# Packing head operands by halves of the sequence, with a block's sums and outputs sent two half steps later

## The chip, the cores and the metric

The kernel runs on one core of a Trainium2 chip. The metric is the device time of one execution in microseconds (us). The core has a matrix engine (TensorE, PE in the profile, with its weight loads apart as PEld), a vector engine (VectorE, DVE), a scalar engine (ScalarE, ACT), a further vector engine (GpSimd, POOL) and a synchronisation engine (SyncE, SP), which in this kernel issues all DMAs. Each engine has its own instruction stream, executed in order.

## The reference

Four residual layers, attention and Fourier mixing in turn, on x of 2048 rows by 640 columns, all in float32. Attention has 32 heads of 20 columns and a sliding window of 256 keys:

```
def _A_ref(x, wqkv, wo):
    H = 32; Dh = D // H; W = 256
    qkv = transpose((x @ wqkv).reshape(B, S, 3, H, Dh), 2, 0, 3, 1, 4)
    q, k, v = qkv[0], qkv[1], qkv[2]
    scores = einsum("bhqd,bhkd->bhqk", q, k) * (Dh ** -0.5)
    mask = (i - j >= 0) & (i - j < W)
    p = softmax(where(mask, scores, -1e9), axis=-1)
    o = einsum("bhqk,bhkd->bhqd", p, v)
    return transpose(o, 0, 2, 1, 3).reshape(B, S, D) @ wo

x = x + _A_ref(_layernorm(x), wqkv, wo)
x = x + _B_ref(_layernorm(x), dft matrices)   # real part of a DFT over both axes
x = x + _A_ref(_layernorm(x), wqkv, wo)
x = x + _B_ref(_layernorm(x), dft matrices)
```

## The kernel before

The sequence is cut into 16 blocks of 128 rows and into four quarters of 512. The 32 heads are cut into 8 quads of four. An attention layer has three parts. `before_heads` normalizes and transposes x and makes the values and the first projections. `heads` (L648) runs 128 steps, one for each quad and block. `after_heads` ends the output projection.

Projected queries and keys go to a DRAM tensor, `qk_d` (L566), as a high and a low part, 512 KB for each piece of 128 projected columns by one quarter. `pack` (L624) brings them back in the layout that the heads read, into `qp` and `kp`. Both are double buffers, by the quad's parity. For one quad and one quarter it makes 12 DMAs, 6 into `kp` and 6 into `qp`: 20 rows each, in two parts of 512 columns, 80 KB. `heads` issues them three to a step, over four steps (L834). The list `due` (L770) says in which step a pack begins: for quads 1 to 6, every four steps, 8 steps before the blocks of that quarter are first read.

A step t of `heads` does, in two half steps z = 0, 1 (two heads each):

- `s_head` for block s = t + 10: scores with the query on the rows (L673), to which DVE adds the mask and takes the largest of each row (L678, into `mc`);
- `t_pair` for block t: scores with the key on the rows (L701), then the exponential on ACT (L711) and two masks on POOL (L717, L721);
- `pv` for block v = t - 1: the product with the values (L736), copied to `ou` by ACT (L745);
- a piece of other matrix work, `fill`: a projection of a later quad, or from step 97 on a first part of the output projection (both L274).

The largest scores reach `t_pair` as a further row of its operand `qp`. Every four steps, in the half step z = 1 of a step t = 2 mod 4, `m_rows` (L683) transposes them (L686), ACT copies them to `mt` (L689), and at the end of that half step the code has SP send two DMAs `qp<-mt` (L691). They hold the rows of four blocks of 128. The rows of blocks 4 to 7 of a quad ("u1" below) stand two steps ahead of the quad's first, and `t_pair` reads them first in the quad's step 2; those of blocks 8 to 11 ("u2") stand in step 2 and are read first in step 6. Both leave four steps.

`finish` (L749) ends a group of four blocks of a quad. In half steps after it, `post` lets it send the softmax sums to `sm` (L755) and the raw output to `o_d` (L756), take the reciprocal on DVE (L758), and store that to `r_d` (L761). The numbers are `at` (L754). `ou` is a double buffer; it is written again five steps after its group has ended.

SP's order is the order of the program's code. SP waits in it where a DMA needs the result of an engine (`mt` of ACT, `sm` and `o_d` of ACT, `r_d` of DVE, `qk_d` of POOL), or needs an earlier DMA to have landed. Other DMAs of SP in the heads are `vq<-v_d` (L663, values), `x<-wqk` (L542, weights), `rr<-kr` and `rr<-ki` (L1459, a check of the Fourier matrices that runs beside the heads), and from step 87 on `x<-o_d`, `rr<-r_d` (L900, L906) and `big<-x` (L1012, the residual, which DVE adds at L1038).

Of the kernel before, what the change touches and what calls it, by code (L numbers as in the profile page):

```python
# [16 lines left out]
P = 128  # L17
# [5 lines left out]
NQ = H // 4  # L23
NSB = 4
# [49 lines left out]
class Net:  # L74
# [546 lines left out]
        self.prepare(4)  # L621


    def pack(self, quad, sb):  # L624

        todo = []
        cols = slice(sb * 512, (sb + 1) * 512)
        for c in range(160 * quad // P, -(-160 * (quad + 1) // P)):
            while self.slot is not None and c > 1 and (c, sb) not in self.packable:
                self.flush(("qk", c, sb))  # L630
                if self.heavy:
                    self.relieve()
                self.tick()

        def put(d, src):
            self.nc.sync.dma_start(d.bitcast(F32), src)

        for kind in (1, 0):
            for e in range(2):
                r0 = 160 * quad + 80 * kind + 40 * e  # L640
                dst = (self.qp, self.kp)[kind][quad % 2].rearrange("p (z s) -> p z s", z=2)
                for part, l in enumerate(((0, 1, 0), (0, 0, 1))[kind]):
                    b = 64 * e + 20 * part
                    src = self.qk[l, r0:r0 + 40, cols].rearrange("(z r) s -> r z s", z=2)
                    todo.append(lambda d=dst[b:b + 20, :, cols], src=src: put(d, src))
        return todo

    def heads(self, xsrc, xdst):  # L648
# [7 lines left out]
        def defer(d, fn):  # L656
            later.setdefault(now[0] + d, []).append(fn)
# [91 lines left out]
        def finish(quad, bk):  # L749
            ou = ous.pop((quad, bk))  # L750
            sm = pool.tile([P, 16], F32, name="sm", tag="sm")
            rc = pool.tile([P, 16], F32, name="rc", tag="rc")
            cols = slice(bk * 512, (bk + 1) * 512)
            at = (2, 9, 11) if quad < NQ - 1 else (1, 5, 6)  # L754
            self.post(at[0], lambda: nc.sync.dma_start(sm, ou[0:P:32, :]))  # L755
            self.post(at[0], lambda: nc.sync.dma_start(  # L756
                self.od[4 * quad:4 * quad + 4, :, cols].rearrange("h r s -> (h r) s"), ou))
            self.post(at[1], lambda: nc.vector.reciprocal(out=rc, in_=sm))  # L758

            def store():  # L760
                nc.sync.dma_start(  # L761
                    self.rd[bk, 4 * quad:4 * quad + 4, :].rearrange("h (a b) -> (h a) b", b=16), rc)
                self.post(2 if quad < NQ - 1 else 0, lambda: self.stored.add((quad, bk)))
            self.post(at[2], store)
# [4 lines left out]

        due = [(16 * q + (4 * j - AHEAD if q < NQ - 1 else LAST_DUE[j]),  # L770
                ((-(-160 * (q + 1) // P) - 1) * NSB + 2 * (j // 2) + 2) * per_piece, q, j)
               for q in range(1, NQ) for j in range(NSB)]
        self.xsrc = xsrc
        self.out = self.partials(xsrc)
        self.rest = self.late(xdst)
# [17 lines left out]
        def fill(n):  # L793

            k, size = 0, 1
            while k < size:
                r = more()
                if r == 0 and k == 0:
                    continue
                if r != 1:  # L800
                    return
                k += 1
                if k == 1:
                    left = self.left + 1
                    size = -(-left // max(1, round(left / n)))
            if self.left == 0:
                more()
                if self.lead:
                    relieve()
                elif self.heavy:  # L810
                    self.heavy.sort(key=lambda h: h[0] not in ROLES["m"])
                    self.relieve()
# [5 lines left out]
        for step in range(-LEAD, steps + 1):  # L818
# [11 lines left out]
            if due and s >= due[0][0]:  # L830
                while done[0] < due[0][1]:
                    fill(15)
                q, j = due.pop(0)[2:]
                for i, f in enumerate(self.pack(q, j)):  # L834
                    defer(i // 3, f)
                for f in later.pop(step, []):
                    f()
# [847 lines left out]
```

## Time and profile before

| | |
|---|---|
| time, median of 3 runs | 1399.29 us (1399.02 to 1400.3) |
| the profiled execution | 1401.8 us, its span 1400.1 us |
| steps of the heads, first attention layer | 163.3 to 541.2 us |
| steps of the heads, second attention layer | 852.8 to 1230.4 us |
| busy share of the span | PE 93%, DVE 70%, ACT 54%, POOL 51% |
| DMA, mean | 187 GB/s |
| DMAs `kp<-qk_d` and `qp<-qk_d` | 384 and 384, 80 KB each |

The busy shares are means over stages with different limits. The heads are 54% of the span, and a quad of 16 steps there takes 43.5 to 48.7 us where nothing but projections runs beside it (quads 1 to 5). Times below are from the span's start. In a line of the profile, `A <-B` names the buffer written and the one read, "x24" a count, and "<-" behind a wait what ended it. Q behind an engine's name (SPq) is its sequencer, where DMAs are issued.

### The profile page before, as it was taken

How to read it: one execution, taken by the hardware profiler on the slowest of the kernel's cores; microseconds unless marked ns; L12 is line 12 of the kernel's file. 1: busy time of each engine (PE TensorE's matmuls, PEld its weight loads, DVE VectorE, ACT ScalarE, POOL GpSimd, SP SyncE). 2: the span in 40 equal slices, each digit the busy share in tenths (PEclk: the TensorE clock that was granted, in tenths of full speed). 3: DMA queues.
4: the chain of work that ended last, by engine and by line, in shares of the span. 5: the costliest groups of instructions: out<-in, count | busy, mean ns of one | idle time of the engine just before them, and what ended most of it. 6: DMA issues, size and time to landing. Idle time of an engine off the chain costs nothing.

```text
span 1400.1 us, 37389 instructions
## 1 busy us (share of the span) xinstructions
PE 1307.4 (93%) x13350; PEld 1007.4 (72%) x13350; DVE 980.9 (70%) x3172; ACT 758.9 (54%) x1651; POOL 713.7 (51%) x1469
## 2 busy tenths in 40 slices
PE   6998999999999889899999999999999988988997
PEld 6898777776766777753689987777676777777445
DVE  6722788787788773877876148887787778658764
ACT  2322378777776564437423225777677755734460
POOL 4221687877777673210323236887777776622000
PEclk9999999999999999999999999999999999999999
DMA  5665576776778875417426646777777787561343
GB/s 192 217 216 158 174 205 201 209 217 206 214 213 245 211 208 143 156 54 241 170 99 193 207 154 195 206 209 202 211 217 214 220 234 219 170 217 46 118 146 144
DMA packets 174295, 261.48 MB, mean 187 GB/s; under 512 B 36306, under 2 KB 85586, under 8 KB 174100
## 3 DMA queue, kind: packets, MB, share of 16 engines
q1 hardware_dynamic: 174100, 259.00, 61.4%
q8 instruction: 108, 1.77, 0.6%
q14 instruction: 87, 0.71, 0.2%
HBM read 175.42 MB, written 82.31 MB: 184 GB/s over the span
## 4 chain that ended last, share of the span: by engine, by line
PE 35%; DMA 7%; DVE 4%; ACT 2%; POOL 2%; SPq 2%; issue 1%; ACTq 0%; DVEq 0%; POOLq 0%
PE banks L274 8%; PE banks L256 7%; PE banks L736 4%; PE banks L1383 3%; PE banks L701 3%; PE banks L1299 3%; PE banks L673 3%; DMA x<-o_d 1%; PE banks L1399 1%; ACT pt L711 1%; DMA qp<-mt 1%; DVE banks L678 1%; DMA big<-x_d 1%; DMA rr<-ki 1%; PE banks L1145 1%
## 5 line engine op out<-in xcount | busy, mean ns | idle before, releaser
L678 DVE CUSTOM_DVE_ANT_0 banks<-banks,mask 128x384 f32<-128x384 f32 (+2 forms) x1024 | 527.1, 557 | 136.3 <-PE banks L673 118.9
L711 ACT ACTIVATE pt<-banks 128x768 f32<-128x768 f32 (+2 forms) x512 | 394.3, 771 | 163.3 <-PE banks L701 115.3
L717 POOL TENSOR_SCALAR_AFFINE_SELECT pt<-pt 128x256 f32<-128x256 f32 x512 | 220.0, 430 | 161.5 <-ACT pt L711 140.3
L274 PE MATMUL banks<-big,wc 64*128 64x512 f32 x1920 | 280.0, 402 | 0.4 <-DVE pt L480 0.4
L701 PE MATMUL banks<-qp,kp 61*128 61x384 f32 (+2 forms) x1024 | 211.2, 383 | 36.8 <-DVE mc L678 18.5
L673 PE MATMUL banks<-kp,qp 60*128 60x384 f32 (+2 forms) x1024 | 212.2, 357 | 10.8 <-DVE mc L678 6.5
L736 PE MATMUL banks<-pt,vq 128*32 128x128 f32 x5760 | 213.0, 279 | 0.9 <-ACT pt L711 0.8
L274 PEld LDWEIGHTS banks<-big,wc 64*128 64x128 f32 x1920 | 196.1, 190 | 20.4 <-ACT x L586 2.7
L721 POOL TENSOR_SCALAR_AFFINE_SELECT pt<-pt 128x256 f32<-128x256 f32 x448 | 188.1, 420 | 0.0
L701 PEld LDWEIGHTS banks<-qp,kp 61*128 61x128 f32 x1024 | 108.8, 187 | 100.9 <-DVE mc L678 66.3
L736 PEld LDWEIGHTS banks<-pt,vq 128*32 128x32 f32 x5760 | 143.4, 110 | 50.3 <-issue 37.1
L673 PEld LDWEIGHTS banks<-kp,qp 60*128 60x128 f32 x1024 | 125.3, 189 | 40.3 <-DVE mc L678 23.4
L678 DVE DVE_READ_ACCUMULATOR2_ANT mc<- 128x1 f32 x1024 | 144.4, 141 | 0.0
L1466 POOL TENSOR_TENSOR rr<-rr 128x228 f32<-128x228 f32 (+3 forms) x113 | 74.7, 666 | 92.0 <-DMA rr<-ki 36.6
L745 ACT ACTIVATE ou<-banks 128x128 f32<-128x128 f32 (+2 forms) x288 | 73.3, 266 | 62.3 <-PE banks L736 56.4
L256 PE MATMUL banks<-qp,big 128*128 128x320 f32 x576 | 98.5, 316 | 1.0 <-POOL qp L382 1.0
L256 PE MATMUL banks<-qp,kp 128*128 128x320 f32 x384 | 88.4, 367 | 10.2 <-ACT big L1118 5.0
L228 POOL TENSOR_TENSOR c<-x,c 128x256 fp32r<-128x256 f32 x128 | 95.5, 753 | 0.0
L256 PEld LDWEIGHTS banks<-qp,big 128*128 128x128 f32 x576 | 88.4, 192 | 1.6 <-POOL qp L382 1.4
L256 PEld LDWEIGHTS banks<-qp,kp 128*128 128x128 f32 x384 | 65.9, 203 | 25.6 <-ACT big L1118 7.6
L274 PE MATMUL banks<-big,big 64*128 64x320 f32 x912 | 79.5, 310 | 0.2 <-ACT mt L689 0.2
L1153 POOL TENSOR_TENSOR rs<-mv,half 128x1 f32<-128x1 f32 x32 | 21.0, 655 | 112.6 <-DVE mv L1152 103.3
(168 smaller groups left out, 1805.9 us busy)
## 6 DMA issues: line engine op xcount, KB each, us to landing
qk_d<-c SPq DMA_DIRECT2D x80, 512.0 KB
kp<-qk_d SPq DMA_DIRECT2D x384, 80.0 KB
qp<-qk_d SPq DMA_DIRECT2D x384, 80.0 KB
o_d<-ou SPq DMA_DIRECT2D x64, 256.0 KB
v_d<-pt SPq DMA_DIRECT2D x16, 768.0 KB
vq<-v_d SPq DMA_DIRECT2D x64, 192.0 KB
rr<-ki SPq DMA_DIRECT2D x40, 228.0 KB
big<-x SPq DMA_DIRECT2D x26, 320.0 KB
```

The source lines that it names most:

```text
L228: eng.tensor_tensor(out=lo[..., c], in0=src[..., c], in1=hi[..., c].bitcast(F32), op=OP.subtract)
L256: self.nc.tensor.matmul(p, x, y, start=n == 0, stop=n == last)
L274: self.nc.tensor.matmul(ps[a], x[r], y[r], start=half + i == 0, stop=half == 1 and i == n - 1, skip_group_check=True)
L673: nc.tensor.matmul(p, qp[quad % 2][b:b + 60, z, qb * P:(qb + 1) * P], kp[quad % 2][b:b + 60, z, k0 * P:(qb + 1) * P], start=True, stop=True)
L678: nc.vector.tensor_tensor_reduce(out=p, in0=p, in1=self.mask[:, 384 - n * P:], scale=1.0, scalar=NEG, op0=OP.add, op1=OP.max, accum_out=mc ...
L701: nc.tensor.matmul(self.banks[:, banks[e], :n * P], kp[quad % 2][b:b + 61, z, kb * P:(kb + 1) * P], qp[quad % 2][b:b + 61, z, kb * P:(kb + ...
L711: nc.scalar.activation(pt[quad, kb][:, 2 * z:2 * z + 2, :n * P], self.banks[:, b0:b1 + 1, :n * P], AF.Exp, scale=SCALE)
L717: nc.gpsimd.affine_select(out=t[:, :, 0:P], in_=t[:, :, 0:P], pattern=[[0, 2], [1, P]], compare_op=OP.is_ge, fill=0.0, base=0, channel_mul ...
L721: nc.gpsimd.affine_select(out=t[:, :, 256:384], in_=t[:, :, 256:384], pattern=[[0, 2], [-1, P]], compare_op=OP.is_gt, fill=0.0, base=0, ch ...
L736: nc.tensor.matmul(self.banks[32 * h:32 * h + 32, bank, :P], vq[:, 96 * (kb % 4) + 21 * h:96 * (kb % 4) + 21 * h + 32], t[:, h, (qb - kb) ...
L745: nc.scalar.activation(ou[:, dst], self.banks[:, bank, src], AF.Copy)
L1466: eng.tensor_tensor(out=t[:, lo:hi], in0=t[:, lo:hi], in1=base.broadcast_to([P, hi - lo, w]), op=op)
```

## The change

`pack` takes a number n of quarters and makes one DMA over all of them. The quads 1 to 6 are packed in two halves of the sequence, each in the place in which its first quarter was packed before; quad 0, packed ahead of the steps, and quad 7 keep quarters. `finish` sends `sm` and `o_d` two half steps later, and takes the reciprocal and stores it one half step later, in all quads but the last.

```
-    def pack(self, quad, sb):
+    def pack(self, quad, sb, n=1):
         todo = []
-        cols = slice(sb * 512, (sb + 1) * 512)
-        for c in range(160 * quad // P, -(-160 * (quad + 1) // P)):
-            while self.slot is not None and c > 1 and (c, sb) not in self.packable:
-                self.flush(("qk", c, sb))
+        cols = slice(sb * 512, (sb + n) * 512)
+        for c, of in ((c, of) for c in range(160 * quad // P, -(-160 * (quad + 1) // P)) for of in range(sb, sb + n)):
+            while self.slot is not None and c > 1 and (c, of) not in self.packable:
+                self.flush(("qk", c, of))
...
-            at = (2, 9, 11) if quad < NQ - 1 else (1, 5, 6)
+            at = (4, 10, 12) if quad < NQ - 1 else (1, 5, 6)
...
-               for q in range(1, NQ) for j in range(NSB)]
+               for q in range(1, NQ) for j in range(0, NSB, 2 if q < NQ - 1 else 1)]
...
-                for i, f in enumerate(self.pack(q, j)):
+                for i, f in enumerate(self.pack(q, j, 2 if q < NQ - 1 else 1)):
```

The `flush` in `pack` is reached neither before nor after: every piece is stored by the time it is packed. So the engines other than SP keep their order, but for the reciprocal on DVE and for one place that follows from the outputs' later store, below.

The first place is SP's stream at the end of quad 1, from the `mt` of quad 2's blocks 0 to 3 (not shown) to the `mt` of its blocks 4 to 7 (the last row). Before:

```order
L636 DMA kp_573<-qk_d 20x2x512 x3
L1459 DMA rr_106<-kr 128x456
L636 DMA qp_122<-qk_d 20x2x512 x3
L663 DMA vq_101<-v_d 128x384
L636 DMA qp_122<-qk_d 20x2x512 x3
L542 DMA x<-wqk 128x640
L755 DMA sm<-ou_104 128x1x16
L756 DMA o_d<-ou_104 128x512
L761 DMA r_d<-rc 128x16
L636 DMA kp_1248<-qk_d 20x2x512 x3
L566 DMA qk_d<-c 128x2x512
L691 DMA qp_122<-mt 2x4x128 x2
```

After, the same stretch:

```order
L1459 DMA rr_106<-kr 128x456
L663 DMA vq_101<-v_d 128x384
L542 DMA x<-wqk 128x640
L636 DMA kp_1248<-qk_d 20x2x1024 x3
L761 DMA r_d<-rc 128x16
L755 DMA sm<-ou_104 128x1x16
L756 DMA o_d<-ou_104 128x512
L566 DMA qk_d<-c 128x2x512
L691 DMA qp_122<-mt 2x4x128 x2
```

Ahead of these two `mt` DMAs stood 19 DMAs, 12 of them packs; now 10 stand there, 3 of them packs, of twice the size. `sm` and `o_d` have moved behind `kp` and behind the reciprocal of the group before them.

The second place is the next stretch, up to the `mt` of quad 2's blocks 8 to 11. After:

```order
L1459 DMA rr_107<-kr 128x456
L636 DMA kp_1248<-qk_d 20x2x1024 x3
L566 DMA qk_d<-c 128x2x512
L636 DMA qp_1249<-qk_d 20x2x1024 x3
L663 DMA vq_99<-v_d 128x384
L636 DMA qp_1249<-qk_d 20x2x1024 x3
L1459 DMA rr_108<-kr 128x456
L761 DMA r_d<-rc 128x16
L755 DMA sm<-ou_105 128x1x16
L756 DMA o_d<-ou_105 128x512
L691 DMA qp_122<-mt 2x4x128 x2
```

This stretch had 12 packs of 80 KB before, and has 9 of 160 KB now. The two kinds of stretch alternate.

The third place is on PE, in step 97 of a layer (quad 6), where the first part of the output projection begins once `o_d` and `r_d` are stored:

```order
 L701 MATMUL banks<-qp_122,kp_573 128x384 x2
 L673 MATMUL banks<-kp_573,qp_122 128x384 x2
-L274 MATMUL banks<-big_5763,big_5764 128x320 x18
 L701 MATMUL banks<-qp_122,kp_573 128x384 x2
 L673 MATMUL banks<-kp_573,qp_122 128x384 x2
```

Each later group of this projection stands one step later, and at the end of the heads one group of nine L256 matmuls more stands behind the last step.

## The prediction

> **What bounds the kernel now.** I read the busy shares first, then who waits for whom on PE, then stretches of one quad each.
>
> ```profile
> PE 1307.4 (93%) x13350; PEld 1007.4 (72%) x13350; DVE 980.9 (70%) x3172; ACT 758.9 (54%) x1651; POOL 713.7 (51%) x1469
> ...
> PE banks L701 <- DMA qp<-mt: 7.1, 5, 3.0
> ...
> PE banks L701 <- DMA qp<-mt: 6.5, 3, 2.6
> ...
> PE banks L701 <- DMA qp<-mt: 1.6, 1, 1.6
> ```
>
> The first row is the page's, the others are PE's waits (us in all, times, longest) in quads 1 to 5 of the first attention layer, in those of the second, and in quad 6 of the first. PE bounds the heads; what it waits for there is the transfer of the largest scores, `mt`. The stretches of quads 1 to 5, both layers:
>
> ```profile
> 207.00:250.80 43.80, 43.04 (x618) 32.68 (x614) 36.83 (x138) 34.01 (x70) 34.42 (x75) 1.00 0.71 204
> 250.80:298.10 47.30, 44.60 (x618) 33.75 (x614) 36.20 (x137) 34.45 (x72) 37.04 (x81) 0.96 0.75 212
> 298.10:342.00 43.90, 42.96 (x616) 32.73 (x612) 36.58 (x138) 33.84 (x70) 34.31 (x75) 1.00 0.70 211
> 342.00:389.80 47.80, 44.35 (x610) 32.94 (x604) 36.92 (x138) 33.87 (x70) 35.96 (x79) 0.96 0.74 211
> 389.80:435.60 45.80, 43.31 (x602) 31.51 (x598) 38.12 (x139) 34.26 (x67) 36.41 (x78) 1.00 0.74 228
> 896.70:940.20 43.50, 42.94 (x616) 32.50 (x612) 36.37 (x137) 34.04 (x70) 35.83 (x83) 1.00 0.71 203
> 940.20:986.50 46.30, 44.59 (x618) 33.81 (x614) 36.36 (x138) 34.58 (x72) 37.07 (x84) 0.96 0.73 206
> 986.50:1033.70 47.20, 44.57 (x618) 33.63 (x614) 36.53 (x138) 33.83 (x70) 36.48 (x85) 0.96 0.79 218
> 1033.70:1077.20 43.50, 42.67 (x610) 31.58 (x606) 36.39 (x137) 33.91 (x70) 35.52 (x83) 1.00 0.72 209
> 1077.20:1125.90 48.70, 45.35 (x600) 33.32 (x596) 38.07 (x140) 34.37 (x67) 36.77 (x79) 0.93 0.73 218
> ```
>
> A row gives the length in us, then busy us of PE, PEld, DVE, ACT and POOL, the granted clock, the DMA share and GB/s. Four quads are alike: 43.80, 43.90, 43.50 and 43.50, mean 43.7. The other six take 283.1 us together, 21.0 more than six times that mean. One such stall, in quad 2 of the first layer, on ACT, SP and PE:
>
> ```profile
> 248.61 0.25 ACT L689 ACTIVATE mt<-banks 16x128 fp32r<-16x128 f32 x1
> ...
> 247.50 1.81 SPq L636 DMA_DIRECT2D qp<-qk_d  x3
> 249.36 0.36 SPq L542 DMA_DIRECT2D x<-wqk  x1
> 250.86 0.61 SPq L755 DMA_DIRECT2D sm<-ou  x1
> 251.51 0.48 SPq L756 DMA_DIRECT2D o_d<-ou  x1
> 252.09 0.37 SPq L761 DMA_DIRECT2D r_d<-rc  x1
> 253.02 1.05 SPq L636 DMA_DIRECT2D kp<-qk_d  x3
> 254.17 0.39 SPq L566 DMA_DIRECT2D qk_d<-c  x1
> 254.89 1.22 SPq L691 DMA_DIRECT2D qp<-mt  x2
> ...
> 258.05 0.69 PE L701 MATMUL banks<-qp,kp 61*128 61x384 f32 x2 [2.16 <-DMA qp<-mt]
> ...
> 255.50:266.50 11.00, 8.84 (x97) 6.58 (x95) 6.84 (x25) 6.30 (x13) 5.08 (x13) 0.84 0.81 242
> ```
>
> `mt` was ready at 248.86, and SP came to it at 254.89, a lag of 6.0 us. Of these, 3.7 are issuing (0.45 left of the packs, 0.36, 0.61, 0.48, 0.37, 1.05, 0.39), the other 2.3 are waits. PE idled 2.16 us, so **a lag of 3.9 us would have cost nothing**. Behind the stall the clock fell: 0.84 over 11.0 us is 1.8 us more. 2.16 and 1.8 make 3.9, near the 3.6 by which this quad exceeds 43.7. So SP's stream is the limit, through `mt` alone.
>
> The clock can be read another way. The Trainium skill's page "TensorE: Matmul & The Clock Gate", Part 1, has the gate fall after an idle window of about 3.4 us; by that a stall of 2.16 us would cost only itself, and the removable time would be 7.1 + 6.5 = 13.6 us in place of 21.0. The row with 0.84 speaks against it, and the sum goes by the rows.
>
> **The change part by part.**
>
> *Fewer packs.* The rows of the change show 19 DMAs ahead of the `mt` of blocks 4 to 7 before, 12 of them packs, and 10 now, 3 of them packs. The price of one:
>
> ```profile
> L636 SPq DMA_DIRECT2D kp<-qk_d x384: 273/336/1382, 56.5 to 1177.4; - x192
> ...
> L566 SPq DMA_DIRECT2D qk_d<-c x80: 359/387/2012, 42.6 to 1146.3; - x80
> ...
> kp<-qk_d SPq DMA_DIRECT2D x384, 80.0 KB
> ...
> qk_d<-c SPq DMA_DIRECT2D x80, 512.0 KB
> ```
>
> The three numbers are least, median and largest ns of one issue. An 80 KB pack costs 336 and a 512 KB store 387, so a pack of 160 KB is taken at 0.34 us; it lies between the two. Six quads lose 24 of 48 packs each in two layers, 288 of 768: 97 us of issuing on SP, 2.0 us in each four steps of some 10.9. That time is on the path only through the lag.
>
> *The lag now, blocks 4 to 7.* The three packs ahead of `mt` need no engine's result of that moment, so SP can issue them early; its gate is `r_d`, whose reciprocal stands three half steps, 4.1 us at 43.7 / 32 = 1.37 each, ahead of the copy to `mt`. From the gate: 0.37 + 0.61 + 0.48 + 0.39 = 1.9 us of issuing, with the 2.3 us of waits kept 4.2. The lag is 0.1 us; with twice the waits 2.4. Both are under 3.9, so the stalls at step 2 of a quad go: **-21.0 us**, bounds 0 and -21.0.
>
> *The lag now, blocks 8 to 11.* Their `mt` stands at the end of the packs. 16 DMAs take 9 x 0.34 + 2 x 0.40 + 0.39 + 0.34 + 0.37 + 0.61 + 0.48 = 6.1 us (`vq` taken as a pack), and the `mt` pair ahead 1.2: 7.3 of 10.9. But the transfers bunch. Four steps now hold 12 x 160 KB of packs, two `qk_d` of 512, and about 0.8 MB of others (`o_d`, `vq` with 128 x 384 x 4 bytes, a check or two): 3.7 MB, and the next four steps 0.8. The most that a stretch of the heads shows is
>
> ```profile
> 449.40:465.50 16.10, 13.79 (x205) 11.39 (x201) 10.20 (x39) 9.13 (x18) 10.60 (x22) 0.89 0.94 289
> ...
> L1459 SPq DMA_DIRECT2D rr<-kr x36: 327/402/1470, 184.3 to 759.2; - x36
> ...
> o_d<-ou SPq DMA_DIRECT2D x64, 256.0 KB
> ...
> rr<-kr SPq DMA_DIRECT2D x36, 228.0 KB
> ```
>
> 289 GB/s at a share of 0.94. At that rate 3.7 MB take 12.8 us, 1.9 over their four steps, so this lag is 0 to 1.9 us, under 3.9. I take **+2.0** for a few short waits; bounds 0 and the slower rival below.
>
> *Sums and outputs later.* From `sm`'s place to the reciprocal there are now six half steps (8.2 us) in place of seven, and from `o_d`'s to the next writing of `ou` seven in place of nine. What waited before:
>
> ```profile
>   DVE rc L758: 2.4, 5
> ```
>
> DVE waited 2.4 us in five of 64 reciprocals, where SP lagged; no such wait of ACT for `o_d` stands among its waits. The lag that goes, up to 6.0 us, is more than the one or two half steps given up. Cost 0, bounds -2.4 and +2.4; it is hidden by DVE's 30% of idle time.
>
> *The output projection's first part one step later.*
>
> ```profile
> 438.97 1.48 PE L274 MATMUL banks<-big,big 64*128 64x320 f32 x18
> ...
> 541.45 1.14 PE L256 MATMUL banks<-big,big 128*128 128x320 f32 x6
> 542.43 0.60 PE L256 MATMUL banks<-big 128*128 128x320 f32 x3
> ...
> DVE big L1038 <- DMA big<-x: 1.4, 1, 1.4
> ...
> DVE big L1038 <- DMA big<-x_d: 2.6, 1, 2.6
> ```
>
> Step 97 loses 1.48 us of PE work; behind the last step nine L256 more take 1.6 (541.45 to 543.03). If step 97 shortens in full this is 0, if not +1.6 a layer: I take **+1.5** for both, bounds 0 and +3.2. DVE's first addition of the residual waited 1.4 and 2.6 us for its load and held PE; the addition comes a step later, 2.9 us, and the load doesn't: **-3.0**, bounds 0 and -4.0.
>
> *Sum.* -21.0 + 2.0 + 1.5 - 3.0 = -20.5 us: from the profiled execution's 1401.8 (span 1400.1) to 1381.3. The median of the runs, 1399.29, is 2.5 below that execution, so I predict **1379**.
>
> **The rivals.**
>
> *Half of it stays.* SP's 2.3 us of waits grow with the larger transfers, and the `mt` of blocks 4 to 7 still lags by 4 to 5 us in some quads. For: SP does wait on landings,
>
> ```profile
> SPq L755 <- DMA rr<-kr: 5.3, 5, 2.2
> ```
>
> Against: 9 of 19 DMAs are gone from ahead of it. Half of 21.0 and no gain at the residual: -10.5 + 3.5 = -7, 1392.
>
> *The change doesn't do what it says.* If the lag is made by bytes in flight, not by issues, it stays, since the bytes are the same: 1399 to 1402 with the moved matmuls. Against: 3.7 of the 6.0 us were issuing.
>
> *Slower: the bunched packs hold up the `mt` of blocks 8 to 11.* Place: step 6 of quads 0 to 5, 12 in all. Price: 4.1 us each, as in the quad of 47.80, so 49 us; with -21.0 + 1.5 that gives 1399 + 30 = 1429. It decides from a lag of 3.9 us. It would come so if a pack, with its 20 rows, runs on 10 of the 16 DMA engines: 1920 / 10 + 1800 / 16 = 305 KB on each of these, at 289 / 16 = 18.1 GB/s 16.9 us, 6.0 over the four steps. Against: in the row 255.50:266.50 these engines would have had 96 + 1700 / 16 = 202 KB (12 packs of 80 KB in its 2.66 MB) in 11.0 us at a share of 0.81, so they could do 22.7 GB/s, and 305 KB take 13.4 us, 2.5 over. The Trainium skill's page "DMA: Bandwidth & Descriptors", "Why a DMA increments its semaphore by 16 and not by 1", has such a rule: a DMA takes the largest number of engines up to 16 that divides its outer sizes, the lowest-numbered ones. No row of this profile shows the engines apart, so this keeps a chance.
>
> **How the numbers follow.** The forecast gets 0.66, half of it 0.14, no effect 0.09, the slower rival 0.11. The low end takes -21.0, -4.0, the 1.6 us of quad 6, and 1.8 us of clock behind each of these three: -32, 1367. The high end takes in the rival that keeps half and most of no effect, and leaves the slower one out: 1367 to 1398. A measurement of this kernel tells 0.2%, 2.8 us, from no change: faster 0.80, same 0.09, slower 0.11.
>
> **What would show it.** Right: all ten stretches near 43.7 us at a clock of 1.00; PE's wait for `qp<-mt` under 4 us in all; 480 packs; in SP's stream `mt` issued within 2 us of the copy. L1038's wait for its load gone. Wrong: waits of L701 for `qp<-mt` at step 6 in place of step 2, a DMA share over 0.95 in every second four steps, ACT's L745 waiting for `o_d<-ou`, or more than 5 us of DVE waiting for `sm`.

## The result, and the profile after

The changed kernel takes 1413.65 us (median of 20 runs, 1401.78 to 1423.27), the kernel before 1403.11 us (median of 20 runs, 1397.51 to 1415.8). The ratio is 1.0053, 95% interval 1.0031 to 1.0075: **slower by half a per cent**, where 1379 was predicted. The difference is small, but the interval doesn't contain 1, and e9 below repeats it. The profiled execution of the change took 1420.27 us, span 1418.5, so it lies 6.6 above its own median.

The page of the changed kernel, busy shares and the DMA queue (packets, MB, share of 16 engines):

```profile
PE 1315.4 (93%) x13350; PEld 1008.8 (71%) x13350; DVE 979.2 (69%) x3172; ACT 759.3 (54%) x1651; POOL 710.1 (50%) x1469
...
q1 hardware_dynamic: 159700, 258.98, 62.7%
```

The averages hardly moved. The waits did (us in all, times, longest), after:

```profile
DVE rc L758 <- DMA sm<-ou: 30.9, 18, 3.9
...
ACT ou L745 <- DMA o_d<-ou: 24.5, 14, 3.6
...
PE banks L701 <- DVE mc L678: 40.8, 54, 3.8
```

PE's wait for `qp<-mt`, 15.2 us in nine places before, is not among its waits any more. In its place DVE waits for `sm` (2.4 us before), ACT for `o_d` (nothing before), and PE for DVE, 18.5 us before:

```profile
PE banks L701 <- DVE mc L678: 18.5, 33, 2.6
```

Stretches of the changed kernel (columns as in the prediction): quads 1 to 5 of the first layer as a whole and of the second, then quad 5, which grew most, and quad 6, of the first layer and of the second.

```profile
207.50:446.40 238.90, 222.43 (x3042) 164.47 (x3038) 184.45 (x686) 170.77 (x349) 177.83 (x387) 0.96 0.76 203
907.30:1145.80 238.50, 221.87 (x3040) 164.05 (x3036) 183.41 (x686) 170.77 (x349) 180.56 (x409) 0.97 0.75 204
...
395.10:446.40 51.30, 45.74 (x602) 33.50 (x598) 38.44 (x139) 34.47 (x67) 35.20 (x77) 0.93 0.71 184
446.40:502.20 55.80, 49.77 (x748) 40.13 (x744) 43.55 (x150) 32.27 (x62) 37.43 (x81) 0.97 0.78 220
...
1092.60:1145.80 53.20, 46.05 (x600) 33.47 (x596) 38.47 (x140) 34.36 (x67) 35.46 (x78) 0.94 0.70 183
1145.80:1198.90 53.10, 47.97 (x750) 38.80 (x746) 43.63 (x150) 32.40 (x62) 37.56 (x81) 1.00 0.83 231
```

The same two stretches of quads 1 to 5 before:

```profile
207.00:435.60 228.60, 218.26 (x3042) 163.61 (x3038) 184.65 (x686) 170.43 (x349) 178.14 (x385) 0.99 0.73 213
896.70:1125.90 229.20, 220.12 (x3040) 164.85 (x3036) 183.71 (x686) 170.72 (x349) 181.68 (x409) 0.97 0.74 211
```

Quads 1 to 5 were to take about 19 us less and took 19.6 more (457.8 to 477.4). Quad 6 took 8.0 less (58.9 and 58.0 before, 55.8 and 53.1 now). Of the other 6.8 us of the span's 18.4, 2.9 and 3.3 lie behind the last step of the two layers, by the records, where in each nine more matmuls of the output projection stand now. The bytes per second fell, 203 and 204 for 213 and 211, though the packs are larger.

One new stall, in quad 4 of the first layer. The timeline of SP, DVE, ACT and PE (start, busy us, instruction; in brackets the idle time before it and what ended it):

```profile
351.31 1.60 SPq L636 DMA_DIRECT2D qp<-qk_d  x3
353.01 0.35 SPq L663 DMA_DIRECT2D vq<-v_d  x1
353.65 2.02 SPq L636 DMA_DIRECT2D qp<-qk_d  x3
356.58 0.34 SPq L761 DMA_DIRECT2D r_d<-rc  x1
358.65 0.62 SPq L755 DMA_DIRECT2D sm<-ou  x1
360.13 0.34 SPq L756 DMA_DIRECT2D o_d<-ou  x1
360.94 1.38 SPq L691 DMA_DIRECT2D qp<-mt  x2
...
364.81 0.25 DVE L758 RECIPROCAL rc<-sm 128x16 f32<-128x16 f32 x1 [3.85 <-DMA sm<-ou]
...
365.31 0.34 ACT L745 ACTIVATE ou<-banks 128x127 f32<-128x127 f32 x2 [3.26 <-DMA o_d<-ou]
...
365.64 0.69 PE L701 MATMUL banks<-qp,kp 61*128 61x384 f32 x2 [3.28 <-DVE mc L678]
```

What SP waited for in 350 to 361 us, and the stretch behind the stall:

```profile
SPq L636 <- DMA qk_d<-c: 1.8, 2, 1.1
SPq L755 <- DMA qp<-qk_d: 1.7, 1, 1.7
SPq L761 <- DMA rr<-kr: 0.8, 1, 0.8
SPq L756 <- DMA qp<-qk_d: 0.8, 1, 0.8
...
364.80:371.60 6.80, 5.96 (x49) 4.60 (x51) 4.08 (x16) 3.06 (x8) 4.95 (x8) 0.50 0.77 223
```

SP is to issue `sm`, whose data has long been there, and waits 1.7 us for a pack to land, with which `sm` has nothing to do. The pack is the one issued at 351.31. Behind it stand `vq`, `r_d` and five more packs: `sm` is the eighth DMA after it. By the trace's records that pack landed at 358.59, 0.06 us before `sm` was issued. In these records this holds for all of SP's DMAs, 1687 before and 1399 after: each signals its end on one of eight semaphores in rotation, and never were more than seven under way when another was issued. **SP waits until the DMA eight places earlier has landed.** A late `sm` stops DVE in its order for 3.85 us, DVE holds up `mc`, PE waits 3.28, and the clock is 0.50 over the next 6.8 us. The late issue isn't all of it: `sm` itself took 6.1 us to land here, where 3.9 was the median before.

Over quads 1 to 5, SP's time in issuing fell from 351 to 252 us by the trace's records. The rows of its waits for transfers add up to 57.5 us in 128 waits before and 169.3 in 237 after. Of the whole span, before:

```profile
SPq L636 <- DMA kp<-qk_d: 6.5, 26, 0.4
...
SPq L761 <- DMA qp<-qk_d: 3.8, 9, 0.8
```

After:

```profile
SPq L636 <- DMA kp<-qk_d: 33.6, 64, 1.4
...
SPq L755 <- DMA qp<-qk_d: 19.0, 21, 2.3
...
SPq L761 <- DMA qp<-qk_d: 16.7, 17, 2.6
```

So 99 us of issuing were saved and 112 us of waits for landings came. The packs land later: by the records, 8.4 us (median) after their issue for `qp` and 4.9 for `kp`, where those of 80 KB took 4.5 and 3.4. The transfers beside them also do: `sm` 5.4 for 3.9, `r_d` 6.4 for 3.5.

### The profile page after: what moved, and what is told of

It is laid out like the page before. It is cut to its first block, busy times and chain, and to the rows that moved or that the text cites. A ratio compares the mean times of both kernels' runs of the same rounds, so it can differ in the third digit from the quotient of the medians.

```text
span 1418.5 us, 37024 instructions
## 1 busy us (share of the span) xinstructions
PE 1315.4 (93%) x13350; PEld 1008.8 (71%) x13350; DVE 979.2 (69%) x3172; ACT 759.3 (54%) x1651; POOL 710.1 (50%) x1469
## 3 DMA queue, kind: packets, MB, share of 16 engines
q1 hardware_dynamic: 159700, 258.98, 62.7%
## 4 chain that ended last, share of the span: by engine, by line
PE 35%; DMA 6%; DVE 4%; POOL 2%; ACT 2%; issue 2%; SPq 1%; POOLq 0%; DVEq 0%; ACTq 0%
PE banks L274 8%; PE banks L256 7%; PE banks L736 4%; PE banks L701 3%; PE banks L1383 3%; PE banks L1299 3%; PE banks L673 3%; DMA sm<-ou 2%; DVE banks L678 1%; PE banks L1399 1%; DMA rr<-ki 1%; ACT pt L711 1%; POOL pt L717 1%; PE banks L1145 1%; DMA qk_d<-c 1%
## 5 line engine op out<-in xcount | busy, mean ns | idle before, releaser
L717 POOL TENSOR_SCALAR_AFFINE_SELECT pt<-pt 128x256 f32<-128x256 f32 x512 | 216.6, 424 | 171.0 <-ACT pt L711 154.4
L736 PE MATMUL banks<-pt,vq 128*32 128x128 f32 x5760 | 216.2, 280 | 2.8 <-ACT pt L711 1.5
L673 PE MATMUL banks<-kp,qp 60*128 60x384 f32 (+2 forms) x1024 | 208.5, 355 | 10.9 <-DVE mc L678 7.8
L721 POOL TENSOR_SCALAR_AFFINE_SELECT pt<-pt 128x256 f32<-128x256 f32 x448 | 184.1, 411 | 0.0
L673 PEld LDWEIGHTS banks<-kp,qp 60*128 60x128 f32 x1024 | 121.7, 190 | 41.2 <-DVE mc L678 25.9
L256 PE MATMUL banks<-qp,big 128*128 128x320 f32 x576 | 100.0, 319 | 1.0 <-POOL qp L382 1.0
L256 PE MATMUL banks<-qp,kp 128*128 128x320 f32 x384 | 89.7, 370 | 10.4 <-ACT big L1118 4.9
L256 PEld LDWEIGHTS banks<-qp,big 128*128 128x128 f32 x576 | 89.7, 194 | 1.6 <-POOL qp L382 1.4
L256 PEld LDWEIGHTS banks<-qp,kp 128*128 128x128 f32 x384 | 66.8, 205 | 26.4 <-ACT big L1118 7.5
```

The costliest lines, as they stand in the source:

```text
L256: self.nc.tensor.matmul(p, x, y, start=n == 0, stop=n == last)
L673: nc.tensor.matmul(p, qp[quad % 2][b:b + 60, z, qb * P:(qb + 1) * P], kp[quad % 2][b:b + 60, z, k0 * P:(qb + 1) * P], start=True, stop=True)
L717: nc.gpsimd.affine_select(out=t[:, :, 0:P], in_=t[:, :, 0:P], pattern=[[0, 2], [1, P]], compare_op=OP.is_ge, fill=0.0, base=0, channel_mul ...
L721: nc.gpsimd.affine_select(out=t[:, :, 256:384], in_=t[:, :, 256:384], pattern=[[0, 2], [-1, P]], compare_op=OP.is_gt, fill=0.0, base=0, ch ...
L736: nc.tensor.matmul(self.banks[32 * h:32 * h + 32, bank, :P], vq[:, 96 * (kb % 4) + 21 * h:96 * (kb % 4) + 21 * h + 32], t[:, h, (qb - kb) ...
```

## The experiments

Each kernel was run in five rounds beside the kernel before. "Places" are the half steps at which `sm` and `o_d` are sent, the reciprocal taken, and the reciprocal stored. Waits are us of PE for `qp<-mt`, DVE for `sm`, ACT for `o_d`, in the one profiled execution of each kernel; these executions lie between 7.6 us below (e8) and 8.2 above (e17) the median of their kernel, so small differences between waits say nothing. The letters of the theories are explained in each expectation: A and L blame the packs that stand at once in SP's stream, B and S the shorter way from `sm` and `o_d` to their users, C says that a wait taken away turns up at the next one, D, P and W blame the transfers themselves (their size, their rows, the engines' time).

| kernel | packs | places | ratio to before (95%) | waits |
|---|---|---|---|---|
| before | 80 KB, 3 a step | 2, 9, 11 | 1 | 15.2, 2.4, 0 |
| e9, the change again | 160 KB, 3 a step for 4 steps | 4, 10, 12 | 1.0060 (1.0032 to 1.0088) | 0.7, 30.5, 22.4 |
| e1 | as the change | 2, 9, 11 | 1.0158 (1.0116 to 1.0199) | 1.3, 39.4, 3.3 |
| e2 | as before | 4, 10, 12 | 1.0105 (1.0065 to 1.0145) | 20.5, 9.8, 11.8 |
| e3 | as the change | 4, 12, 14 | 1.0075 (1.0042 to 1.0107) | 7.0, 0, 12.9 |
| e5 | 160 KB, 3 every second step for 8, from 2 steps earlier | 2, 9, 11 | 0.9939 (0.9905 to 0.9973) | 19.5, 0, 0 |
| e6 | as e5 | 4, 10, 12 | 1.0032 (1.0004 to 1.0060) | 10.9, 20.4, 15.1 |
| e7 | 80 KB in rows of 4096 bytes, 3 a step for 8, from 2 steps earlier | 2, 9, 11 | 1.0055 (1.0033 to 1.0077) | 6.6, 3.5, 0 |
| e8 | 80 KB in rows of 2048 bytes, else as e7 | 2, 9, 11 | 1.0066 (1.0046 to 1.0087) | 5.8, 4.9, 0 |
| e10 | as the change | 2, 10, 12 | 1.0105 (1.0056 to 1.0155) | 10.9, 27.3, 17.5 |
| e11 | as e5 | 2, 10, 12 | 0.9921 (0.9885 to 0.9956) | 19.6, 0.6, 0 |
| e12 | 160 KB, 2 a step for 6, from 2 steps earlier | 2, 9, 11 | 0.9916 (0.9887 to 0.9946) | 3.8, 11.5, 0 |
| e13 | as e12, from 4 steps earlier | 2, 9, 11 | 1.0168 (1.0118 to 1.0218) | 22.5, 15.0, 0 |
| e14 | as the change, issued by GpSimd | 4, 10, 12 | 1.0564 (1.0528 to 1.0601) | 0.7, 0, 0.3 |
| e15 | as e12 | 2, 10, 12 | 0.9849 (0.9807 to 0.9891) | 9.1, 2.2, 2.0 |
| e16 | as the change, from 2 steps earlier | 2, 9, 11 | 1.0144 (1.0106 to 1.0182) | 24.2, 0.2, 0 |
| e17 | 160 KB, 2 a step for 6, from the change's place | 2, 9, 11 | 1.0252 (1.0207 to 1.0298) | 2.6, 1.3, 0 |
| e18 | as before | 2, 10, 12 | 1.0034 (1.0006 to 1.0063) | 18.3, 0.2, 0 |
| e19, e15 again | as e12 | 2, 10, 12 | 0.9830 (0.9804 to 0.9855) | 8.6, 4.1, 0.8 |

### Each half of the change alone, and a later reciprocal (e1, e2, e3)

e1 keeps the halves and puts the places back; e2 keeps quarters and takes the new places; e3 is the change with the reciprocal two half steps later still.

```
e1  -            at = (4, 10, 12) if quad < NQ - 1 else (1, 5, 6)
    +            at = (2, 9, 11) if quad < NQ - 1 else (1, 5, 6)
e2  -            at = (2, 9, 11) if quad < NQ - 1 else (1, 5, 6)     (of the kernel before)
    +            at = (4, 10, 12) if quad < NQ - 1 else (1, 5, 6)
e3  -            at = (4, 10, 12) if quad < NQ - 1 else (1, 5, 6)
    +            at = (4, 12, 14) if quad < NQ - 1 else (1, 5, 6)
```

> Halves as in the change, but sm, o_d, the reciprocal and r_d at their old places (2, 9, 11). Theory A (the bunched transfers of a half make SP fall behind at the end of each burst, wherever sm stands in the code): SP comes to sm at about the same time as in the changed kernel, since the last packs still stand ahead of it, and the reciprocal stands half a step earlier: DVE waits 25 to 45 us for sm in all, time 0.3% to 1.2% over before. Theory B (the later place of sm is what costs): sm goes out 2.7 us earlier, DVE waits under 8 us for it, the stalls on mt at step 2 stay away, time 1.0% to 1.5% under before.

> Quarters as before, with sm, o_d, the reciprocal and r_d at the new places (4, 10, 12). Theory A: no bunching; SP lags 3 to 6 us as before, and sm has one half step (1.4 us) less: DVE waits 5 to 20 us for sm, the stalls on mt at step 2 stay, time 0 to 0.8% over before. Theory B: the later place alone costs what the change costs and more, DVE waits 30 us or more for sm, time 1% to 2% over before.

> The change with the reciprocal and the store of r_d two half steps later still (4, 12, 14): sm gets 2.7 us more before DVE asks for it, SP's load stays the same. Theory A and B: the DVE waits for sm fall from 30.9 to under 10 us, and with them the stalls at step 5 of a quad; time 0.5% to 1.5% under the changed kernel. A rival C (the stalls at step 5 come from ACT's wait for o_d or from the mt of blocks 8 to 11, which land just as late, and DVE's wait only stands first): the stalls move to L745 or to L701 behind mt at step 6, time as the changed kernel's within 0.4%.

Either half alone loses, by 1.6% and 1.1%; together they lose 0.5%. So the loss is not that of the later places: with halves these make it smaller. Of the two expectations theory A has the waits right (DVE for `sm` 39.4 us in e1 and 9.8 in e2, where the stalls on `mt` stay), but both kernels lost more than it had (0.3 to 1.2% and 0 to 0.8%); theory B falls with e1. In e1, the waits:

```profile
DVE rc L758 <- DMA sm<-ou: 39.4, 20, 4.4
```

All the halves' gain is there (PE waits 1.3 us for `mt`), and DVE's waits for `sm` take more than that. e3, which doesn't compute the reference's result (where it departs wasn't found) and keeps the number of DMAs, leaves DVE no wait for `sm`; ACT's for `o_d` falls to 12.9, and PE's for `mt` comes back with 7.0. Part of the wait comes out at other DMAs of the stream. The time as a whole stays, but not for that reason: by the records quads 1 to 5 take 466.2 us where the change takes 477.5, much as theories A and B have it, and quad 7 takes 57.3 and 57.4 us where it takes 48.8 and 48.7. In quad 7 PE waits once in each layer for an exponential, first layer and second:

```profile
PE banks L736 <- ACT pt L711: 6.8, 1, 6.8
```

```profile
PE banks L736 <- ACT pt L711: 7.7, 1, 7.7
```

So e3's total doesn't show that a stall moves whole to the next wait. What makes quad 7's stall was not followed.

### Packs spread out, and the later places on top (e5, e6, e11)

e5 begins two steps earlier and issues three packs in every second step, with the places of before. e6 and e11 differ from it in the places only.

```
-        due = [(16 * q + (4 * j - AHEAD if q < NQ - 1 else LAST_DUE[j]),
+        due = [(16 * q + (4 * j - AHEAD - 2 if q < NQ - 1 else LAST_DUE[j]),
...
-                    defer(i // 3, f)
+                    defer((2 if q < NQ - 1 else 1) * (i // 3), f)
```

> Halves, but their 12 DMAs go three in every second step over eight steps, beginning two steps earlier, with sm, o_d, the reciprocal and r_d at their old places (2, 9, 11). SP's issues and the bytes are then even. Theory A: lags of SP stay under 3 us, waits of DVE for sm under 8 us, of PE for mt under 4 us, time 1.0% to 1.8% under before. A rival D (a transfer of 160 KB is itself the cost, since it lands later than two of 80 KB): the waits stay as in the changed kernel, time 0 to 1% over before.

> Packs of 160 KB, three in every second step over eight steps, begun two steps earlier, and the sums and outputs at (4, 10, 12) as in the change. Theory A (SP's queue is the limit, later sums let the qp<-mt transfers pass): PE's wait for qp<-mt falls from 19.5 us of the spread kernel with (2, 9, 11) to under 10, and the time to 1390 to 1398. Theory C (the later places shift the stall to DVE's wait for sm and ACT's for o_d): these waits come back with over 10 us, 1402 to 1412.

> The spread kernel (three packs of 160 KB in every second step, sums sent at 2) with the reciprocal and its store at 10 and 12 in place of 9 and 11. Theory S: no waits for sm there already, so nothing but SP's order changes: r_d goes later, the mt behind it earlier; PE's wait for qp<-mt below 19.5 us, ratio 0.988 to 0.995. Theory C: 0.994 to 1.003.

e5 is faster than before, with the same 160 KB packs, and DVE doesn't wait for `sm` nor ACT for `o_d`. So halves as such don't lose, and theory D falls; it matters how closely they follow each other, and where (e12 to e17 below). It isn't theory A as written either: PE's waits for `mt`, under 4 us by it, are 19.5, and the gain is 0.6% where it had 1.0 to 1.8. With the change's places (e6) the waits come back, as theory C has it:

```profile
DVE rc L758 <- DMA sm<-ou: 20.4, 16, 2.9
...
ACT ou L745 <- DMA o_d<-ou: 15.1, 12, 2.8
```

Here the two half steps that `sm` and `o_d` give up cost 0.9% (0.9939 to 1.0032). With `sm` and `o_d` left at 2, the later reciprocal and store alone (e11) cost nothing: 0.9921, with PE's waits for `mt` as in e5 (19.6).

### The length of a row (e7, e8)

The packs of the change move in rows of 4096 bytes instead of 2048, and their packets took more of the DMA engines' time (62.7% for 61.4%) with the same bytes. e7 and e8 cut each pack of e5 by its two groups of heads, three of 80 KB in a step for eight steps; e8 keeps `qk_d` by quarters in DRAM, so that the same 80 KB move in rows of 2048 bytes.

```
e7  +                    for z in range(2):
    +                        src = self.qk[l, r0 + 20 * z:r0 + 20 * z + 20, cols]
    +                        todo.append(lambda d=dst[b:b + 20, z, cols], src=src: put(d, src))
e8  -        self.qk = dram.tile([2, 2 * D, S], F32, name="qk_d")
    +        self.qk = dram.tile([2, NSB, 2 * D, 512], F32, name="qk_d")
```

> Halves of the sequence, but each pack of 160 KB cut in two by its two groups of heads: 80 KB each, 24 for a half, in rows of 4096 bytes, issued three in a step over eight steps, begun two steps earlier; sums and outputs at (2, 9, 11). Count, size and rate of the packs are those of before; what differs is the length of a row (4096 for 2048 bytes) and the order. Theory P (a row of 4096 bytes costs more than two of 2048): the first queue's share of the 16 engines stays at 62.5 to 65%, all landings are later than before, and the time is 0.5 to 1.5% above that of the kernel of this call that has rows of 2048 bytes. Theory A (the change lost by sending 3.8 MB in four steps, the length of a row is nothing): the two kernels agree within 0.3%, both lie within 0.5% of before (1396 to 1410), and the share is 61.4%.

> As the kernel with packs of 80 KB in rows of 4096 bytes, with one difference: the rows that are packed lie in DRAM by quarters of the sequence, so that the same 80 KB go in rows of 2048 bytes. Theory P: the packets are as before (mean about 105 ns, first queue's share 61 to 62%), the time is 0.5 to 1.5% below its partner's, ratio to before 0.995 to 1.003. Theory A: equal to its partner within 0.3%.

The page's DMA queue, e7 and then e8:

```profile
q1 hardware_dynamic: 162580, 259.00, 61.5%
```

```profile
q1 hardware_dynamic: 174100, 259.00, 62.2%
```

1412.55 and 1413.79 us: the length of a row changes nothing, and theory P falls. The two agree as theory A has it, but both lie outside its range, at 0.6% above before. The Trainium skill's page "Perfetto Trace Analysis", "DMA Optimizations", recommends batching small transfers into larger ones, such as 2 KB into 4 KB or 8 KB, for throughput. It speaks of whole transfers; the row within a transfer of 80 KB is another matter, and there no gain shows, in time or in the queue's share. Against e5, which has half as many DMAs with the same bytes, the two lose 1.2 and 1.3%. That the number of packs makes this is not shown: the last packs of a half also stand a step later in e7 and e8 than in e5. What they lose by shows in PE's wait for the packs themselves, `qp<-qk_d`, 16.7 us in e7 and 15.7 in e8, with e5's at 3.5.

> The change itself, so that it and the others stand against the same runs of before. All theories: 1.003 to 1.0075 of before, 1404 to 1418.

The change, measured again beside these, gave 1.0060, within its bounds.

### Sending the sums early (e10)

```
-            at = (4, 10, 12) if quad < NQ - 1 else (1, 5, 6)
+            at = (2, 10, 12) if quad < NQ - 1 else (1, 5, 6)
```

> The change with one number of its places put back: sums and outputs are sent at half step 2 as before, the reciprocal and its store stay at 10 and 12. From the sending of sm to its use there are then 8 half steps in place of 6. Theory S (the loss of the change is the short way from the sending of sm and o_d, queued behind three packs of 160 KB, to their users): DVE's waits for sm and ACT's for o_d fall from 30.9 and 24.5 us to under 10 together, and the time to 0.985 to 0.995 of before. Theory C (whatever stall is taken away turns up at the next wait, since the SP queue and the packs as a whole are late): the waits for qp<-mt or qp<-qk_d take their place, and the time stays at 1.002 to 1.008.

1.0105, and the waits stayed:

```profile
DVE rc L758 <- DMA sm<-ou: 27.3, 16, 4.5
...
ACT ou L745 <- DMA o_d<-ou: 17.5, 9, 4.4
```

Theory S in this form falls. Theory C has the waits (PE's for `mt` are 10.9 us, 0.7 in e9), but the time lies above its range too. By the records, in the two groups of a quad that meet the burst, `sm` was issued 6.2 and 6.4 us ahead of the moment at which DVE asks for it, against 5.5 and 4.3 in the change: of two half steps, 2.7 us, that it was to gain, SP gave it about one. And it took 6.7 and 6.5 us to land, 5.8 in the change. An earlier place in the program helps a DMA little that stands in a stream which is late.

### Density against place (e12, e13, e16, e17)

e12 issues two packs a step over six steps, begun two steps earlier than the change; e13 is the same begun four steps earlier, e17 begun where the change begins; e16 keeps three packs a step over four steps, begun two steps earlier. All have (2, 9, 11).

```
e12  +        due = [(16 * q + (4 * j - AHEAD - 2 if q < NQ - 1 else LAST_DUE[j]),
     +                    defer(i // (2 if q < NQ - 1 else 3), f)
e13  +        due = [(16 * q + (4 * j - AHEAD - 4 if q < NQ - 1 else LAST_DUE[j]),
     +                    defer(i // (2 if q < NQ - 1 else 3), f)
e16  +        due = [(16 * q + (4 * j - AHEAD - 2 if q < NQ - 1 else LAST_DUE[j]),
e17  +                    defer(i // (2 if q < NQ - 1 else 3), f)
```

> The spread kernel with (2, 9, 11), but two packs of 160 KB in each step over six steps instead of three in every second step over eight. Theory A (what counts is how many packs stand at once ahead of a small transfer): lags of mt and landings of sm not above those of the spread kernel, ratio 0.990 to 0.996. If the bytes in a step decide (320 KB in a step here, 240 KB there, 480 KB in the change), the waits lie between: ratio 0.997 to 1.005 with DVE waits for sm of 5 to 20 us.

> The same, begun four steps earlier than in the change instead of two, so that the six steps lie elsewhere against the blocks. Theory A: the landing of packs is less tight, PE's wait for qp<-qk_d and kp<-qk_d (6.8 us in the spread kernel) goes, 0.988 to 0.996. If the place of the packs against the sums decides: ratio differs from its partner's by over 0.5% either way.

> Three packs of 160 KB in each of four steps as in the change, but begun two steps earlier, with (2, 9, 11) as before. If the density of the packs decides (theory L): as the kernel with halves alone, 1.012 to 1.020. If their place against the sums and the mt decides: under 1.005, as in the kernels that begin two steps earlier and spread them.

> Two packs of 160 KB in each of six steps, begun where the change begins them, with (2, 9, 11). If the density decides (theory L): 0.990 to 0.998, as its partner begun two steps earlier (0.992). If the place decides: over 1.005. PE's wait for the packs themselves can come up here, since the last of a half are issued two steps later than in the change.

e16 came as density has it (1.0144), e12 at the fast end (0.9916), but e13 and e17 are as sparse as e12 and lose 1.7% and 2.5%. Neither density nor place decides alone. PE's waits say which user comes too early, e16, e13 and e17 in this order:

```profile
PE banks L701 <- DMA qp<-mt: 24.2, 14, 3.7
```

```profile
PE banks L701 <- DMA qp<-mt: 22.5, 14, 2.6
```

```profile
PE banks L673 <- DMA qp<-qk_d: 16.8, 9, 2.9
...
PE banks L673 <- DMA sm<-ou: 8.7, 2, 4.5
```

In e16 and e13 it is `mt` again, and in e17 PE waits for the packs, whose last are issued two steps later than in the change. (The last row is of this kind too: L673 doesn't read `sm`, and by the records a pack lands just as the longer of the two waits ends.) The landings are alike in all four (5.5 to 5.9 us on average over SP's DMAs in quads 1 to 5, by the records; 5.7 in the change). What differs, as I read these waits, is which DMA stands last behind the packs, and how much time it has; no run takes this apart further.

### The packs off SP's stream (e14)

```
-            self.nc.sync.dma_start(d.bitcast(F32), src)
+            (self.nc.sync if self.slot is None else self.nc.gpsimd).dma_start(d.bitcast(F32), src)
```

> The change with the packs of the heads issued by GpSimd instead of SP; bytes, rows, places in the program and (4, 10, 12) stay. Theory L (SP lets only eight DMAs be under way: each issue waits until the one eight issues earlier has landed; packs of 160 KB that take 8 us to land hold these places, and what stands behind them, sm, o_d, r_d and mt, is issued late): SP's waits for landings in quads 1 to 5, 176 us in the change, fall under 60, DVE's waits for sm (30.9 us) and ACT's for o_d (24.5) under 10 together. If issuing on GpSimd costs nothing else, 0.980 to 0.992 of before; what GpSimd's masks lose by it shows as PE waits for pt and comes on top. Theory W (it is the bandwidth of the engines that the bunched packs take): landings of sm stay at 5 us and more, and its waits above 15 us.

The time is 1.0564, far above the range. The waits are as theory L has them. SP's waits for landings in quads 1 to 5 add up to 5.9 us in seven waits (169.3 in the change), and the largest there are now for engines, which means that SP comes early. Waits of SP in quads 1 to 5 of the first layer, then those of PE there:

```profile
SPq L761 <- DVE rc L758: 60.0, 18, 4.9
SPq L691 <- ACT mt L689: 47.6, 15, 4.4
...
PE banks L736 <- POOL pt L717: 19.8, 43, 1.3
...
PE banks L701 <- DMA qp<-mt: 0.7, 1, 0.7
```

DVE waits for `sm` nowhere and ACT 0.3 us for `o_d`, with the same bytes, the same packs and the same places as in the change. Yet `sm` lands late in this kernel too: 8.1 us on average in the two groups that meet the packs, by the records (5.8 in the change). It is issued at its place, 11.6 and 12.2 us ahead of its use on average, and so that does no harm. So the stalls of the change come from the order of SP's stream with its eight places: landings as late as these stall nothing when SP itself is on time. Theory W, that the engines' time is what the bunched packs take, falls as their direct cause; whether it makes the landings late isn't shown. The Trainium skill's page "Trainium Kernel Development and Optimization", "Key Constraints", says that issuing from several engines only saves the sequencer's issue time; here it also saved 163 us of SP's waits for landings.

What was lost instead stands on GpSimd, busy us and mean ns of one:

```profile
L636 POOL DMA_DIRECT2D kp<-qk_d x192 | 113.9, 595 | 0.1
L636 POOL DMA_DIRECT2D qp<-qk_d x192 | 112.9, 590 | 0.7 <-DMA kp<-qk_d 0.7
```

A pack costs it 0.59 us, 227 us in all, ahead of the masks for which PE then waits, 51.3 us in the whole span (1.4 in the change). These waits are less than the 73 us by which e14 stands above the change; the rest was not followed.

### A version that beats both (e15, e18, e19)

e15 is e12 with the reciprocal and its store one half step later; e19 is the same kernel run again; e18 gives the kernel before the same places.

```
e15  -            at = (2, 9, 11) if quad < NQ - 1 else (1, 5, 6)     (of e12)
     +            at = (2, 10, 12) if quad < NQ - 1 else (1, 5, 6)
e18  -            at = (2, 9, 11) if quad < NQ - 1 else (1, 5, 6)     (of the kernel before)
     +            at = (2, 10, 12) if quad < NQ - 1 else (1, 5, 6)
```

> Two packs of 160 KB in each step over six steps, begun two steps earlier than in the change, sums sent at 2, reciprocal and store at 10 and 12. Theory L: the eleven us of waits for sm of its partner with (2, 9, 11) go, since one half step (1.4 us) more is left for them: 0.984 to 0.991. If a stall that is taken away turns up at the next wait: 0.990 to 0.998.

> The kernel before, quarters and all, with the reciprocal and its store at 10 and 12 in place of 9 and 11, sums sent at 2. If the gain of the kernel with two packs of 160 KB a step and (2, 10, 12) (0.985) comes from the halves and their spreading: 0.995 to 1.003 here. If it comes from the later reciprocal alone: 0.985 to 0.992, with PE's wait for qp<-mt under 8 us (15.2 before).

> Two packs of 160 KB a step over six steps, begun two steps earlier, (2, 10, 12): the same kernel as the one measured at 0.985, so that it stands against the quarters of this call on the same chip. 0.981 to 0.989.

e15 took 1385.34 us, ratio 0.9849, and e19 1384.28, ratio 0.9830 (0.9804 to 0.9855). The quarters gained nothing by the later reciprocal (1.0034), so the gain is that of the halves, spread out, in this place. By the profiled executions e15's span is 12.4 us shorter than that of before, 6.1 of it in quads 1 to 5 and 8.2 in quad 6, where the change gains as much. What PE and its suppliers still wait for in e15:

```profile
PE banks L701 <- DMA qp<-mt: 9.1, 7, 2.3
DVE rc L758 <- DMA sm<-ou: 2.2, 3, 1.1
...
ACT ou L745 <- DMA o_d<-ou: 2.0, 3, 0.9
```

SP itself waits for landings nearly as long as in the change, 159.1 us in 250 waits for 169.3 in 237. The sum of a queue's waits is no price; what stands behind them and how much time it has is.

## Why the prediction was wrong, step by step

- **Fewer packs.** Right: 480 packs, and one of 160 KB costs SP what one of 80 KB did:

```profile
L636 SPq DMA_DIRECT2D kp<-qk_d x240: 273/335/1365, 57.0 to 1194.4; - x120
```

- **The lag of blocks 4 to 7, -21.0.** Right as far as it went. Their `mt` is issued 0 to 2.2 us after the copy, 0.5 on average over ten quads (4.4 before), and PE's waits for it are gone.
- **"With the 2.3 us of waits kept"** is the root of the error. These waits were held constant while the packs doubled, and they are a resource with a price of its own. SP's stream was taken to be made of issues, 0.34 us each, with the landings as a remainder; when all eight places are taken it moves at a DMA per eighth of a landing time. An estimate from the records: the first four steps of each eight of quads 1 to 5 had 20.1 DMAs with a mean landing of 4.1 us before, 20.1 x 4.1 / 8 = 10.3 us, just within the 10.9 that four undisturbed steps take. After, they hold 13.1 DMAs that land in 7.2: 11.8 us, over it. The next four steps hold 16.6 at 4.5, 9.3 us. It is in these next four that the time is lost: by the records they take 13.2 us on average (11.1 before), the first four 10.7 (11.8 before). SP's waits for landings, the remainder of the forecast, rose from 57.5 to 169.3 us. The 97 us of issuing that the forecast took off SP were real (99) and were given back whole.
- **The lag of blocks 8 to 11, "0 to 1.9 us, under 3.9", +2.0.** This step failed in size. It was 3.6 to 6.9 us, 5.0 on average. The step compared 3.7 MB with 289 GB/s. The stream holds up at 204 GB/s and a mean DMA share of 0.76, because SP runs out of places. That doesn't acquit the DMA engines: the share is a mean over 16 of them. By the records a pack, before and after, adds to its semaphore once within about half a us of its issue and then ten times as it lands, where a DMA of 128 rows adds sixteen times and `sm`, with 4 rows at its source, once and then four times. This looks as if ten engines carried a pack, which is the condition of the slower rival. The packs' packets are 0.33 of the 0.76; on ten engines they would fill these to about 0.33 x 16 / 10 + 0.43 = 0.96, an estimate that no run here tests.
- **Sums and outputs later, "cost 0, bounds -2.4 and +2.4".** The loss stands in this term: it priced `sm`, `o_d` and their waits at nothing. The later places alone didn't make it, since e1, without them, waits 39.4 us for `sm` and loses 1.6%. The argument was that the lag that goes is more than the half steps given up. That holds for `mt` of blocks 4 to 7, but `sm` and `o_d` of the groups that meet the burst stand right behind its packs, and there the lag grew. DVE's and ACT's waits are 30.9 and 24.5 us, and PE's behind DVE rose by 22.3. The later places do cost where there is no burst (e2 1.1%, e6 against e5 0.9%), and they help beside one (1.0158 to 1.0053).
- **The residual's load, -3.0, and the moved matmuls, +1.5.** Right in direction: L1038 waits for no load, and quad 6 took 8.0 us less in the two layers. Some 3.0 of these are the 18 matmuls of step 97 (1.48 us by the prediction's row, in two layers), and the stretches behind the last step grew by 2.9 and 3.3 us. If all of that growth is theirs, the moved matmuls cost about 3, near the upper bound of 3.2. How the rest of quad 6's gain divides wasn't measured.
- **The rivals.** The slower one had nearly the place (it named step 6 of a quad; DVE's stalls stand in steps 5 and 13) and the lag (over 3.9 us; 5.0 measured), but the wrong victim: PE doesn't wait for `mt` there, DVE and ACT wait for `sm` and `o_d`. Its 30 us were nearly three times the 10.5 between the medians. What it blamed, ten engines for a pack, stays open, as said above. "Half of it stays" had the resource, SP's waits on landings, without following it to the other DMAs of the stream. Of the signs of being wrong, ACT waiting for `o_d` and DVE over 5 us for `sm` came as written; a DMA share over 0.95 in every second four steps didn't (at most 0.92 by the records).

The 1379 itself, 20 us below before, is about what e15 and e19 reach against theirs (20 and 24), with the packs spread and the sums sent early. That is near the forecast's size, not its working: 21.0 us were to come from quads 1 to 5, and by the profiled executions these give 6.1 and 10.5, quad 6 8.2 and 10.0, with `mt` still waited for.

What stays open: why a pack of 160 KB into `qp` lands 8 us after its issue when it goes in threes (twice the bytes, 1.9 times the time for `qp`, 1.5 for `kp`). A pack in more rows, which might reach more DMA engines, wasn't tried. And the 2.5% by which two steps of place divide e12 from e13 are read from the waits, not predicted from a rule.

## What to carry to other kernels

A queue that issues in order and admits a fixed number of transfers, eight here, has two prices, its issue time and its landing time divided by that number; fewer and larger transfers lower the first and can raise the second. Before merging transfers, list the small ones behind them, which engines wait for each and with how much lead, and give those the lead or the packs the gaps. When a wait is taken away and the time stays, read which DMA stands next in the same stream, and compare stretch by stretch: a loss elsewhere can hide the gain, as quad 7 does in e3.

## What was not expected of the hardware

- Rows of 4096 and 2048 bytes, in packs of 80 KB, cost alike: 61.5% and 62.2% of the DMA engines' time for the same 259 MB, 1412.55 and 1413.79 us.
- Transfers that have nothing to do with the packs land later while larger packs are under way: `r_d` 6.4 us for 3.5, `sm` 5.4 for 3.9, at a DMA share of 0.75 to 0.76 for 0.73 to 0.74.
- A stall of 3.3 us was followed by 6.8 us at half the granted clock. That is 3.4 us more, as long as the stall itself. It isn't the rule: by the changed kernel's clock records, seven other stalls of 1.2 to 3.8 us in the heads were followed by 3.4 us at half clock, and others, the longest of 2.1 us, by none.
- Issuing a pack of 160 KB held GpSimd for 0.59 us on average; a pack held SP for 0.36 in the changed kernel.
